# A two-layer MLP on one core: the opening reordered (smaller first loads, one more dummy matmul, half-width first tiles)

## The chip, the cores and the metric

The kernel runs on one core of one Trainium2 chip. The metric is the device time of one execution in microseconds (us). The profiled span is shorter than that time by about 1.8 us (132.8 against 134.6 in the same execution). Ratios below are the mean time of one kernel's fast runs over the mean time of the other's fast runs of the same rounds, on the same chip, so they are not quite the ratio of the medians that are quoted.

## The reference

```python
# x: (1, 2048, 640), w1: (640, 1728), w2: (1728, 640), all bf16
def reference(x, w1, w2):
    h = jnp.einsum("bsd,df->bsf", x, w1)
    h = jax.nn.silu(h)
    return jnp.einsum("bsf,fd->bsd", h, w2)
```

## The kernel before

The first layer needs x transposed (640 on the partitions). Rows are taken in four chunks of 512. The first chunk is loaded plainly and transposed on TensorE by matmuls against an identity; the other three come by transposing DMAs, which are issued some 1.3 us apart and land 2.8 us after their issue (from the trace), but have time. The 1728 columns of w1 (padded) give 14 tiles of 128, so the first layer is 4 x 14 groups of five 512-wide matmuls (280), each followed by a sigmoid on ScalarE and a multiplication on VectorE. The second layer is 448 matmuls. Before the first x arrives, five dummy matmuls on zeros keep TensorE occupied (1.19 to 3.50 us in the trace). PSUM is the memory that the matmuls write their results to. These are the parts that matter:

```python
w1_groups = [(0, 2), (2, 8), (8, FT)]      # weight tiles per DMA
N_WARM_MM = 5

@block.sync
def _(sp):
    hj = JB // 2                            # JB = 4 blocks of 128 rows
    sp.dma_start(out=x0_sb[:, 0:hj, :], in_=x0_v[:, 0:hj, :]).then_inc(sem_x0[0], 16)
    ...
    sp.wait_ge(sem_x0[1], 16)
    for gi in range(2, len(w1_groups)):
        load_w1_group(gi)
    ...
@block.scalar
def _(act):
    act.dma_start(out=x0_sb[:, hj:JB, :], in_=x0_v[:, hj:JB, :]).then_inc(sem_x0[1], 16)
    for gi in range(2):                     # w1 groups 0 and 1
        act.dma_start(...).then_inc(sem_w1[gi], 16)
    ...
@block.tensor
def _(pe):
    pe.wait_ge(sem_z, 1)
    for i in range(N_WARM_MM):              # dummies on zeros
        pe.matmul(ps1[:, NB1 - 1, :], lhsT=z_sb[:, 0:P], rhs=z_sb[:, :], start=True, stop=True)
    pe.wait_ge(sem_init, N_INIT)
    for j in range(JB):                     # 4 x 5 transposes
        if j % 2 == 0:
            pe.wait_ge(sem_x0[j // 2], 16)
        ...
    for sc in range(NSC):
        if sc == 0:                         # all four blocks copied out of PSUM
            pe.wait_ge(sem_tpc_v, JB)
            pe.wait_ge(sem_tpc_a, JB)
        ...
        for ft in range(FT):
            ...                             # 5 matmuls of 512 columns into ps1[:, buf, :]
```

## Time and profile before

Median 134.91 us in the first four runs. The profiled execution took 134.6 us.

| part of the profiled span (132.8 us) | us |
|---|---|
| up to the first real matmul | 7.55 |
| from there to the first matmul of the second layer | 61.64 |
| second layer, first to last matmul start | 60.80 |
| last matmul, copies, last store | 2.8 |

The page of the profile gives TensorE (PE) as the bound. The first line lists busy time per engine, the next two are the chain of work that ended last. PEld is TensorE's loading of weights, DVE VectorE, ACT ScalarE, POOL GpSimd, and SP the engine that issues most DMAs; L266 is line 266 of the kernel.

```profile
PE 126.5 (95%) x739; PEld 64.7 (49%) x753; DVE 51.6 (39%) x76; ACT 41.0 (31%) x77; POOL 1.6 (1%) x9
...
PE 94%; DMA 3%; issue 1%; DVE 0%; ACT 0%
PE ps L266 46%; PE ps L303 46%; DMA x_sb<-in_x_dram 3%; PE ps L240 2%; DVE xT_sb L384 0%; ACT o_sb L366 0%
```

A share of 95% seems to leave nothing. But busy is not the same as fast. The timeline of PE alone, over the first 13 us of the kernel before (start in us, duration, what, count, and in brackets the idle time ahead of it and what ended it), shows two gaps:

```profile
1.19 2.31 PE L224 MATMUL ps<-z_sb 128*128 128x512 bf16 x5 [1.19 <-DVE z_sb L379]
4.64 2.29 PE L240 MATMUL ps<-ident,x_sb 128*128 128x128 bf16 x20 [1.14 <-DMA x_sb<-in_x_dram]
7.55 5.68 PE L266 MATMUL ps<-xT_sb,w_sb 128*128 128x512 bf16 x20 [0.61 <-DVE xT_sb L384]
```

Dummies, then 1.14 us without x, then transposes, then 0.61 us until the last copy of transposed x is out of PSUM. The timeline of the weight loads (PEld, one per matmul) shows what the busy share hides. Each line is a load or a run of loads with no idle between:

```profile
8.79 0.15 PEld L266 LDWEIGHTS ps<-xT_sb,w_sb 128*128 128x128 bf16 x1 [0.28 <-issue]
9.21 0.15 PEld L266 LDWEIGHTS ps<-xT_sb,w_sb 128*128 128x128 bf16 x1 [0.28 <-issue]
9.64 0.15 PEld L266 LDWEIGHTS ps<-xT_sb,w_sb 128*128 128x128 bf16 x1 [0.28 <-issue]
10.05 1.39 PEld L266 LDWEIGHTS ps<-xT_sb,w_sb 128*128 128x128 bf16 x7 [0.26 <-issue]
```

Up to 9.64 the loads are 0.43 us apart, from 10.05 on about 0.216 us. The matmuls follow the same beat. So the first real matmuls ran at half speed although the clock row of the page reads full speed throughout. The packed trace does hold the step, in records that no view prints: its first record of the granted clock begins at 10.02 us, and the row counts as full whatever has no record. "Cold" and "released" below mean these two spacings.

The DMAs at the beginning (size, time from issue to landing; the two x loads were issued at 0.73 and 0.74 us):

```profile
x_sb<-in_x_dram SPq DMA_DIRECT2D x1, 320.0 KB, 3.8
x_sb<-in_x_dram ACTq DMA_DIRECT2D x1, 320.0 KB, 4.1
w_sb<-in_w_dram ACTq DMA_DIRECT2D x1, 320.0 KB, 4.6
```

### The profile page before, as it was taken

To read this page: it belongs to the slowest core of one execution; us is meant where nothing else is said; L and a number is where in the kernel's file an instruction comes from. 1 tells how busy PE (TensorE), PEld (TensorE's weight loads), DVE (VectorE), ACT (ScalarE), POOL (GpSimd) and SP (SyncE) were. 2 spreads that over 40 slices of the span, in tenths; PEclk is the share of its full clock that TensorE was granted. 3 is DMA by queue.
4 is the path that set the end of the run, shared out by engine and by line. 5 is a ranking of instruction groups with operands and counts; after the bars stand their busy time and mean duration, and the time that the engine had idled before them with its cause. 6 is when DMAs were issued, how large, how long until landed. Compare 5 with 4: busy or idle time off the path is not lost.

```text
span 132.8 us, 1833 instructions
## 1 busy us (share of the span) xinstructions
PE 126.5 (95%) x739; PEld 64.7 (49%) x753; DVE 51.6 (39%) x76; ACT 41.0 (31%) x77; POOL 1.6 (1%) x9
## 2 busy tenths in 40 slices
PE   6689999999999999999999999999999999999992
PEld 1624444444444444444445555555555555555461
DVE  0315666666666666666662222222012222220121
ACT  2525555555555555555550000000000000000001
POOL 4000000000000000000000000000000000000000
PEclk9999999999999999999999999999999999999999
DMA  4995444899300000000000111011111110111103
GB/s 104 354 362 140 102 102 97 274 378 141 73 2 0 0 5 2 0 0 0 0 0 5 49 49 49 14 35 54 49 49 49 49 54 7 42 49 49 54 0 99
DMA packets 15016, 9.78 MB, mean 74 GB/s; under 512 B 8800, under 2 KB 15008, under 8 KB 15008
## 3 DMA queue, kind: packets, MB, share of 16 engines
q1 hardware_dynamic: 13152, 7.97, 22.3%
q10 hardware_dynamic: 1856, 1.70, 4.0%
q8 instruction: 6, 0.10, 0.3%
q14 instruction: 2, 0.02, 0.0%
HBM read 5.08 MB, written 2.62 MB: 58 GB/s over the span
## 4 chain that ended last, share of the span: by engine, by line
PE 94%; DMA 3%; issue 1%; DVE 0%; ACT 0%
PE ps L266 46%; PE ps L303 46%; DMA x_sb<-in_x_dram 3%; PE ps L240 2%; DVE xT_sb L384 0%; ACT o_sb L366 0%
## 5 line engine op out<-in xcount | busy, mean ns | idle before, releaser
L266 PE MATMUL ps<-xT_sb,w_sb 128*128 128x512 bf16 x274 | 61.5, 384 | 0.9 <-DVE xT_sb L384 0.6
L303 PE MATMUL ps<-w_sb,hT_sb 128*128 128x512 bf16 (+1 forms) x440 | 60.6, 298 | 0.4
L393 DVE TENSOR_TENSOR hT_sb<-ps,sig_sb 128x512 bf16<-128x512 f32 x56 | 38.7, 691 | 24.6 <-ACT sig_sb L342 24.6
L303 PEld LDWEIGHTS ps<-w_sb,hT_sb 128*128 128x128 bf16 x448 | 34.5, 98 | 26.7
L266 PEld LDWEIGHTS ps<-xT_sb,w_sb 128*128 128x128 bf16 x280 | 27.6, 99 | 34.6 <-issue 1.7
L342 ACT ACTIVATE sig_sb<-ps 128x512 bf16<-128x512 f32 x56 | 33.4, 597 | 29.1 <-PE ps L266 29.1
L406 DVE CAST o_sb<-ps 128x512 bf16<-128x512 f32 x14 | 9.7, 692 | 42.9 <-PE ps L303 42.9
L354 ACT CAST o_sb<-ps 128x128 bf16<-128x128 f32 x14 | 3.7, 266 | 49.2 <-PE ps L303 49.2
L384 DVE CAST xT_sb<-ps 128x256 bf16<-128x256 f32 x4 | 1.7, 425 | 4.6 <-PE ps L240 4.3
L224 PE MATMUL ps<-z_sb 128*128 128x512 bf16 x5 | 2.3, 629 | 1.2 <-DVE z_sb L379 1.2
L240 PE MATMUL ps<-ident,x_sb 128*128 128x128 bf16 x20 | 2.3, 309 | 1.1 <-DMA x_sb<-in_x_dram 1.1
L418 DVE CAST o_sb<-ps 128x1024 bf16<-128x1024 f32 x1 | 1.2, 1225 | 5.3 <-PE ps L303 5.3
L240 PEld LDWEIGHTS ps<-ident,x_sb 128*128 128x128 bf16 x20 | 2.1, 143 | 2.0 <-issue 2.0
L366 ACT CAST o_sb<-ps 128x256 bf16<-128x256 f32 x1 | 0.4, 372 | 7.3 <-PE ps L303 7.3
L331 ACT CAST xT_sb<-ps 128x384 bf16<-128x384 f32 x4 | 1.9, 479 | 1.6 <-PE ps L240 1.5
L325 ACT ACT_TABLE_LOAD x1 | 1.3, 1283 | 2.4 <-issue 2.4
L224 PEld LDWEIGHTS ps<-z_sb 128*128 128x128 bf16 x5 | 0.6, 135 | 2.0 <-DVE z_sb L379 1.2
L153 POOL MEMSET w_sb<- 128x640 bf16 x1 | 0.6, 632 | 0.0
L379 DVE MEMSET z_sb<- 128x256 uint32 x1 | 0.3, 272 | 0.9 <-PEq L435 0.9
L150 POOL MEMSET w_sb<- 128x320 bf16 x1 | 0.4, 366 | 0.0
L140 POOL TENSOR_SCALAR_AFFINE_SELECT ident<-ident 128x128 bf16<-128x128 bf16 x1 | 0.3, 294 | 0.2 <-POOL ident L138 0.2
L325 ACT ACTIVATE warm_sb<-warm_sb 128x32 f32<-128x32 f32 x1 | 0.2, 230 | 0.0
(6 smaller groups left out, 0.7 us busy)
## 6 DMA issues: line engine op xcount, KB each, us to landing
out_dram<-o_sb SPq DMA_DIRECT2D x14, 160.0 KB, 1.8
w_sb<-in_w_dram SPq DMA_DIRECT2D x1, 1120.0 KB, 9.6
w_sb<-in_w_dram ACTq DMA_DIRECT2D x1, 960.0 KB, 7.2
w_sb<-in_w_dram SPq DMA_DIRECT2D x1, 960.0 KB, 7.0
w_sb<-in_w_dram SPq DMA_DIRECT2D x1, 880.0 KB, 6.3
x_sb<-in_x_dram SPq DMA_DIRECT2D x1, 320.0 KB, 3.8
x_sb<-in_x_dram ACTq DMA_DIRECT2D x1, 320.0 KB, 4.1
w_sb<-in_w_dram ACTq DMA_DIRECT2D x1, 320.0 KB, 4.6
```

The lines of the kernel that those rows point to most:

```text
L224: pe.matmul(ps1[:, NB1 - 1, :], lhsT=z_sb[:, 0:P], rhs=z_sb[:, :], start=True, stop=True,)
L240: ins = pe.matmul(tp_views[wv][:, sl, :], lhsT=x0_sb[:, j, dt * P:(dt + 1) * P], rhs=ident[:, :], start=True, stop=True,)
L266: ins = pe.matmul(ps1[:, buf, :], lhsT=w1_sb[:, dt, ft * P:(ft + 1) * P], rhs=xT_sb[:, dt, sc * SCH:(sc + 1) * SCH], start=(dt == 0), stop ...
L303: ins = pe.matmul(ps2[:, b2, c0:c0 + ncol], lhsT=hT_sb[:, ft, st * P:(st + 1) * P], rhs=w2_sb[:, ft, d0:d0 + ncol], start=(ft == 0), stop= ...
L325: act.activation(out=warm_sb[:, :], in_=warm_sb[:, :], func=ACT.Sigmoid)
L331: act.copy(out=xT_sb[:, TPV:DT, j * P:(j + 1) * P], in_=tp_views[wv][:, s0_:s0_ + (DT - TPV), :],).then_inc(sem_tpc_a, 1)
L342: act.activation(out=sig_sb[:, buf, :], in_=ps1[:, buf, :], func=ACT.Sigmoid,).then_inc(sem_act1, 1)
L354: act.copy(out=o_sb[:, ob, DA:D], in_=ps2[:, b2, c0:c0 + ncol]).then_inc(sem_ev_a, 1)
L384: dve.tensor_copy(out=xT_sb[:, 0:TPV, j * P:(j + 1) * P], in_=tp_views[wv][:, s0_:s0_ + TPV, :],).then_inc(sem_tpc_v, 1)
L393: dve.tensor_tensor(out=hT_sb[:, ft, sc * SCH:(sc + 1) * SCH], in0=ps1[:, buf, :], in1=sig_sb[:, buf, :], op=ALU.mult,).then_inc(sem_dve1, 1)
L406: dve.tensor_copy(out=o_sb[:, ob, 0:DA], in_=ps2[:, b2, c0:c0 + ncol]).then_inc(sem_ev_v, 1)
L418: dve.tensor_copy(out=o_sb[:, obA:obA + 2, 0:DA], in_=ps2[:, bA_, 0:2 * DA].rearrange("p (t c) -> p t c", t=2),).then_inc(sem_ev_v, 1)
```

## The change

The intent is to start the real matmuls earlier and to keep PE occupied from the start. Core of the diff, with lines shortened and joined (the loops over `units` on ScalarE and VectorE follow the one on PE; cut):

```diff
-    w1_groups = [(0, 2), (2, 8), (8, FT)]
+    w1_groups = [(0, 2), (2, 4), (4, 8), (8, FT)]
+    N_W1_ACT = 1                       # ACT issues group 0 only, SP the others
+    W1_BIG = 2
+    HN = SCH // 2
+    N_SPLIT_FT = 2                     # first two weight tiles in 256-column halves
+    units = [(0,0,0,HN), (0,1,0,HN), (0,0,HN,HN), (0,1,HN,HN), then 512-wide ...]
-    N_WARM_MM = 5
+    N_WARM_MM = 6
+    TP_BANKS = {0: (1, 0), 1: (1, 8), 2: (0, 8), 3: (1, 0)}   # transposes of block 3 reuse block 0's bank
+            pool.memset(z_sb[:, SCH // 2:SCH], 0.0).then_inc(sem_z, 1)   # POOL clears half of the zeros
-            sp.dma_start(out=x0_sb[:, 0:hj, :], in_=x0_v[:, 0:hj, :]).then_inc(sem_x0[0], 16)
+            for j in range(0, JB, 2):  # ACT likewise with j = 1, 3
+                sp.dma_start(out=x0_sb[:, j, :], in_=x0_v[:, j, :]).then_inc(sem_x0[j // 2], 16)
-            sp.wait_ge(sem_x0[1], 16)
+            sp.wait_ge(sem_x0[0], 32)
-                    pe.wait_ge(sem_tpc_v, JB)
-                    pe.wait_ge(sem_tpc_a, JB)
+                    jneed = (c0 + n - 1) // P + 1     # first halves need two blocks only
+                    pe.wait_ge(sem_tpc_v, jneed); pe.wait_ge(sem_tpc_a, jneed)
```

## The prediction

> **What bounds the kernel now.** TensorE. The engine summary has PE busy 126.5 of 132.8 us (95%); the chain of waits is 46% first-matmul line, 46% second-matmul line, 3% the DMA of the first x rows, 2% their transposes. From 7.55 to 130.2 us the chain shows only matmuls with 0.05 us issue gaps. So only the first 7.55 us and the tail can shrink; the change touches the beginning.
>
> **The beginning, from the timeline.** Five dummy matmuls run 1.19 to 3.50. PE then idles 1.14 us for x (two 320 KB loads, issued at 0.73, land 3.8 and 4.1 us later). Twenty transposes run 4.64 to 6.95, PE idles 0.61 us for the last copy, and real matmuls start at 7.55. The first six start 0.43 us apart, those after 10.05 us 0.216: 1.3 us lost to a slow PE. The clock row does not show it (it reads full); the spacing does. [...]
>
> **What the change does.**
> 1. x comes as four 160 KB loads, two per queue; the first two should land at about 3.6 us. In the window table the DMA has moved some 336 KB by 3.3 us and then runs at about 360 GB/s.
> 2. Warm-up starts 0.1 us earlier (memset halved over DVE and POOL) and gets a sixth matmul (+0.43 us): it ends at about 3.65, where x lands. The 1.14 us gap goes.
> 3. Transposes, still 20 at about 0.107 us: 3.65 to 5.8.
> 4. The first two weight tiles are multiplied in 256-column halves; the first half needs only the copies of blocks 0 and 1 (ready about 5.5), so the 0.61 us gap goes. Ten matmuls of 512 become twenty of 256; at 0.1 us each a weight load (98 ns) just hides. Cost under 0.1 us.
> 5. The first w1 load (landed about 5.9 before) becomes the likely last input: real matmuls start at about 6.0 instead of 7.55. The second group lands about 6.6, needed after 8; later loads have microseconds of slack.
>
> **Sum.** Start: -1.55 us. [...] Split: +0.1. All is on the critical path, since PE is gapless afterwards. Total about -2.5 us (-1.2 to -3.5). From 134.91: **132.4 us**, range **131.4 to 133.5**. The 2% limit lies at 132.2, so it is close: faster by over 2% 0.42, within 2% 0.57, slower 0.01.
>
> **What would show each step.** The chain's DMA and transpose part falls from 4.5% to about 3%; first real matmul at 5.8 to 6.3; no PE idle over 0.3 us after 1.2; fewer than six cold-spaced 512-column equivalents; the steady part unchanged (384 and 298 ns mean per matmul group; second-matmul phase 61.0 us).
>
> **What would make it wrong.** x or w1 landing late (more loads, 0.4 to 0.5 us issue each): start at 6.5 to 7, a gain of 1 us only. The clock released no earlier than 10 us: a gain of about 0.5 us, since work moved before it runs at half speed. Or released before 5 us: the transposes speed up too, and 131.5 is possible. The unchanged kernel's runs come in two values (134.6 and 135.2), which may be this release falling at different times; it blurs so small a difference.

The start (-1.55 us) and the split (+0.1) come to -1.45; the other 1.0 us of the total of 2.5 was the estimate of how much less would be lost to cold matmuls, and it rested on what no trace shows.

## The result, and the profile after

The changed kernel takes 132.12 us in the median (131.8 to 132.68, 11 runs) against 134.53 (133.4 to 135.24, 16 runs). The ratio is 0.9828 with a 95% interval of 0.9799 to 0.9856. Executions over 1.5% slower than the fastest of the same kernel are left out of the means. The interval straddles 0.98; the gain of about 2.3 us itself is clear of noise. The scatter shrank from 1.8 to 0.9 us. A later repeat of the unedited changed kernel (e9) gave 131.98 us and 0.9843.

The page of the kernel after, the same lines as above:

```profile
PE 125.2 (96%) x750; PEld 65.0 (50%) x764; DVE 51.5 (40%) x78; ACT 41.0 (32%) x79; POOL 1.9 (1%) x10
...
PE 94%; DMA 3%; issue 1%; ACT 0%
PE ps L334 46%; PE ps L297 46%; DMA x_sb<-in_x_dram 3%; PE ps L263 1%; ACT o_sb L395 0%
```

The page hardly differs. The timelines of PE and of its weight loads do:

```profile
1.10 2.74 PE L245 MATMUL ps<-z_sb 128*128 128x512 bf16 x6 [1.10 <-POOL z_sb L158]
4.13 1.79 PE L263 MATMUL ps<-ident,x_sb 128*128 128x128 bf16 x20 [0.29 <-DMA x_sb<-in_x_dram]
5.96 10.33 PE L297 MATMUL ps<-xT_sb,w_sb 128*128 128x256 bf16 x56
```

```profile
4.10 1.14 PEld L263 LDWEIGHTS ps<-ident,x_sb 128*128 128x128 bf16 x15 [1.17 <-issue]
5.45 0.29 PEld L263 LDWEIGHTS ps<-ident,x_sb 128*128 128x128 bf16 x5 [0.21 <-DVE xT_sb L413]
5.93 5.55 PEld L297 LDWEIGHTS ps<-xT_sb,w_sb 128*128 128x128 bf16 x37 [0.18 <-DVE xT_sb L413]
```

The first real matmul starts at 5.96 instead of 7.55 us. The last five transposes need 0.29 us, which is 58 ns each, about half of the cold 107 ns: the speed was released in the middle of the transposes, at 4.77 us by the clock record, and no real matmul was cold. The DMA table after:

```profile
x_sb<-in_x_dram SPq DMA_DIRECT2D x2, 160.0 KB, 3.2
x_sb<-in_x_dram ACTq DMA_DIRECT2D x2, 160.0 KB, 3.2
w_sb<-in_w_dram ACTq DMA_DIRECT2D x1, 320.0 KB, 4.2
```

**Where the time went.** The four parts of the span can be read from the timelines of every profiled execution. The second layer takes 60.80 us in each and the end 2.8, so the span is 63.6 plus the first two columns. With no cold matmul and no wait the first layer takes 60.43 us (without the halves) or 60.46 us (with them); what exceeds that is the loss. The two anchored runs e7 and e12 are left out of the table; their first layer takes 60.46 us too, after a start at 12.47 and 11.63 us.

| kernel | first real matmul (us) | first layer (us) | of it lost: cold | of it lost: waiting for w1 | span |
|---|---|---|---|---|---|
| before | 7.55 | 61.64 | 1.2 | | 132.8 |
| after | 5.96 | 60.46 | 0 | | 130.0 |
| e1 before, 8 dummies | 6.70 | 60.80 | 0 | 0.4 | 131.1 |
| e2 after, no dummies | 5.95 | 61.84 | 1.4 | | 131.4 |
| e3 after, no halves | 6.29 | 60.43 | 0 | | 130.3 |
| e4 after, x in two loads | 6.66 | 61.55 | 1.1 | | 131.8 |
| e5 after, 4 dummies | 5.93 | 60.75 | 0.3 | | 130.3 |
| e6 before, x in four loads | 6.89 | 60.92 | 0 | 0.5 | 131.4 |
| e8 after, old w1 groups | 7.27 | 61.17 | 0 | 0.7 | 132.1 |
| e9 after, unedited | 5.94 | 60.46 | 0 | | 130.0 |
| e10 after, 7 dummies | 5.95 | 60.46 | 0 | | 130.0 |
| e11 after, 8 early dummies | 6.17 | 60.72 | 0 | 0.3 | 130.5 |

So of the 2.8 us between the two profiled executions, 1.59 come from the start of the real matmuls and 1.18 from the cold loss. What this sum does not tell is the cause: the transposes, too, run at half or full speed (107 or 58 ns each), so part of the earlier start may itself be the earlier release. That is what the experiments take apart.

### The profile page after: what moved, and what is told of

Same layout as the page of the kernel before. It is cut to its first block, busy times and chain, and to the rows that moved or that the text cites. A ratio compares the mean times of both kernels' runs of the same rounds, so it can differ in the third digit from the quotient of the medians.

```text
span 130.0 us, 1869 instructions
## 1 busy us (share of the span) xinstructions
PE 125.2 (96%) x750; PEld 65.0 (50%) x764; DVE 51.5 (40%) x78; ACT 41.0 (32%) x79; POOL 1.9 (1%) x10
## 4 chain that ended last, share of the span: by engine, by line
PE 94%; DMA 3%; issue 1%; ACT 0%
PE ps L334 46%; PE ps L297 46%; DMA x_sb<-in_x_dram 3%; PE ps L263 1%; ACT o_sb L395 0%
## 5 line engine op out<-in xcount | busy, mean ns | idle before, releaser
L297 PE MATMUL ps<-xT_sb,w_sb 128*128 128x512 bf16 (+1 forms) x284 | 60.3, 371 | 0.3
L421 DVE TENSOR_TENSOR hT_sb<-ps,sig_sb 128x512 bf16<-128x512 f32 (+1 forms) x58 | 39.0, 673 | 22.5 <-ACT sig_sb L371 22.2
L297 PEld LDWEIGHTS ps<-xT_sb,w_sb 128*128 128x128 bf16 x290 | 28.3, 98 | 32.0 <-DVE xT_sb L413 0.2
L371 ACT ACTIVATE sig_sb<-ps 128x512 bf16<-128x512 f32 (+1 forms) x58 | 33.8, 583 | 26.9 <-PE ps L297 26.9
L263 PEld LDWEIGHTS ps<-ident,x_sb 128*128 128x128 bf16 x20 | 1.4, 113 | 1.4 <-issue 1.2
L263 PE MATMUL ps<-ident,x_sb 128*128 128x128 bf16 x20 | 1.7, 246 | 0.4 <-DMA x_sb<-in_x_dram 0.3
```

The source lines that it names most:

```text
L263: ins = pe.matmul(tp_views[wv][:, sl, :], lhsT=x0_sb[:, j, dt * P:(dt + 1) * P], rhs=ident[:, :], start=True, stop=True,)
L297: ins = pe.matmul(ps1[:, buf, 0:n], lhsT=w1_sb[:, dt, ft * P:(ft + 1) * P], rhs=xT_sb[:, dt, col0:col0 + n], start=(dt == 0), stop=(dt == ...
L371: act.activation(out=sig_sb[:, buf, 0:n], in_=ps1[:, buf, 0:n], func=ACT.Sigmoid,).then_inc(sem_act1, 1)
L421: dve.tensor_tensor(out=hT_sb[:, ft, col0:col0 + n], in0=ps1[:, buf, 0:n], in1=sig_sb[:, buf, 0:n], op=ALU.mult,).then_inc(sem_dve1, 1)
```

## The experiments

**Theory A.** A good part of the gain, perhaps half, is an earlier release of PE's speed, and it comes earlier because the change closes most of the idle gap of 1.14 us ahead of the transposes. How much work the release needs, and when it is then due, the author assumed; that is not shown by the runs. **Rival B.** Only the earlier availability of x and w1 counts; the release comes when it comes. Further rivals are named where they arise. The medians of before were 134.17 (e1 to e4), 134.87 (e5 to e8) and 134.05 (e9 to e12), so times are compared by their ratios to before.

### e1: the kernel before with 8 dummies

```diff
-    N_WARM_MM = 5
+    N_WARM_MM = 8
```

> The kernel before with 8 dummy matmuls instead of 5 and nothing else: they fill the 1.14 us in which PE waits for x. Theory A (part of the gain is an earlier release of the PE clock[...]): real matmuls still start at 7.5 to 7.7 us, but they are spaced 0.216 us from the start or nearly so, fewer than 3 of the cold 0.43 us spacings, and the time falls by 0.6 to 1.2 us against before (ratio 0.991 to 0.9955). Rival B (the gain is only the earlier start of the real matmuls; the release comes when it comes): no change or up to 0.1 us slower, six cold matmuls as before.

Measured: 132.90 us (132.69 to 133.35), ratio 0.9896 (0.9857 to 0.9934). One changed number gives 1.3 us, more than half of what the whole change gives. Timeline of PE:

```profile
1.18 3.39 PE L224 MATMUL ps<-z_sb 128*128 128x512 bf16 x8 [1.18 <-DVE z_sb L379]
4.50 1.28 PE L240 MATMUL ps<-ident,x_sb 128*128 128x128 bf16 x20
6.70 2.32 PE L266 MATMUL ps<-xT_sb,w_sb 128*128 128x512 bf16 x10 [0.93 <-ACT xT_sb L331]
9.22 2.12 PE L266 MATMUL ps<-xT_sb,w_sb 128*128 128x512 bf16 x9 [0.20 <-DMA w_sb<-in_w_dram]
```

The twenty transposes take 1.28 us instead of 2.29 and no real matmul is cold (ten in 2.32 us). The real matmuls start at 6.70, which neither theory had said: I had expected 7.5 to 7.7 and had forgotten that released transposes end earlier (0.14 us of the 0.85 us come from an earlier x in this execution). B is refuted. The gain was larger than A's 0.6 to 1.2 us for that reason. The last line shows the next limit: the third weight tile is now waited for.

### e2: the changed kernel without dummies

```diff
-    N_WARM_MM = 6
+    N_WARM_MM = 0
```

> The changed kernel without any dummy matmul. PE's first work is then the transposes at about 4.1 us. Theory A: real matmuls start at 6.2 to 6.5 us, [...]1.0 to 2.2 us of the gain are lost: 133.2 to 134.3. Rival B: the start of the real matmuls alone counts: 132.2 to 132.7.

Measured: 132.89 us (132.14 to 133.51), ratio 0.9881 (0.9839 to 0.9924). Timeline of PE:

```profile
3.86 2.29 PE L263 MATMUL ps<-ident,x_sb 128*128 128x128 bf16 x20 [3.86 <-DMA x_sb<-in_x_dram]
5.95 5.24 PE L297 MATMUL ps<-xT_sb,w_sb 128*128 128x256 bf16 x27
```

The real matmuls start at 5.95 us, the same as with dummies, yet 0.5 to 0.7 us are lost by the ratios and 0.8 by the medians, 1.4 in this profile, all of it as cold matmuls. This is the cleanest separation of the two causes: equal start, different release. The median lies between the two forecasts, below A's 133.2 and above B's 132.7. In the profile the release came 4.9 us after the first PE work (clock record at 8.76 us). That the loss by the medians is smaller than A had said I put down to executions with an earlier release, and to some loss in the changed kernel too; no profile shows either.

### e3: the changed kernel without the halves

```diff
-    N_SPLIT_FT = 2
+    N_SPLIT_FT = 0
```

> The changed kernel without the halves: all first-layer matmuls are 512 wide, so the first waits for the copies of all four x blocks. Both theories: PE idles some 0.5 to 0.6 us between the transposes and the first real matmul, real start at 6.5 to 6.7 instead of 5.96, time 0.4 to 0.6 us above the changed kernel (132.5 to 132.8). If the halves are worth nothing: 132.1.

Measured: 132.32 us (132.11 to 132.81), ratio 0.9851 (0.9815 to 0.9887), against 0.9828 and 0.9843 for the changed kernel: 0.1 to 0.3 us, less than expected and hardly clear of noise. Timeline of PE:

```profile
3.67 1.88 PE L263 MATMUL ps<-ident,x_sb 128*128 128x128 bf16 x20
6.29 4.91 PE L297 MATMUL ps<-xT_sb,w_sb 128*128 128x512 bf16 x22 [0.74 <-ACT xT_sb L362]
```

The expected gap is there (0.74 us), but x landed 0.5 us earlier in this execution than in that of the changed kernel, so the start moved by 0.33 us only. The halves are the smallest part of the change, and their gain is hardly shown.

### e4: the changed kernel with x in two loads

```diff
-            for j in range(0, JB, 2):
-                sp.dma_start(out=x0_sb[:, j, :], in_=x0_v[:, j, :]).then_inc(sem_x0[j // 2], 16)
+            sp.dma_start(out=x0_sb[:, 0:hj, :], in_=x0_v[:, 0:hj, :]).then_inc(sem_x0[0], 16)
             ...   # ACT likewise with blocks 2 and 3; waits for 16 instead of 32
```

> The changed kernel with x loaded as before, in two loads of 320 KB, everything else as changed. If the four smaller loads bring the earlier landing: first x block usable at about 4.5 instead of 4.0, real start at 6.4 to 6.5, time 0.3 to 0.6 us above the changed kernel (132.4 to 132.8), part of it from a gap of 0.7 us in front of the transposes that may delay the clock's release. If it is the first w1 load (landing at 5.9) that sets the start: 0 to 0.1 us.

Measured: 132.57 us over the four fast runs (131.85 to 133.59), ratio 0.987 (0.9811 to 0.9929). By the ratios 0.4 to 0.6 us are lost against the changed kernel, as expected. The median hides two groups: 131.85 and 131.93, and then 133.20 and 133.59, with nothing between; the two runs labelled slow (133.96 and 134.03, granted clock 1.0) lie just above the second. Timeline of PE, from the run at 133.59:

```profile
4.57 2.29 PE L263 MATMUL ps<-ident,x_sb 128*128 128x128 bf16 x20 [0.73 <-DMA x_sb<-in_x_dram]
6.66 4.51 PE L297 MATMUL ps<-xT_sb,w_sb 128*128 128x256 bf16 x24
```

Here the transposes are cold, the start is 0.7 us later, and half-width matmuls stay cold until 8.89 us (clock record). An idle gap of 0.73 us (0.94 by the spacing: the last dummy starts 2.11 us after the first and takes 0.43, the transposes start 3.48 after it) went with this late release, against 0.29 us and a release at 4.77 in the changed kernel. Why the runs fall into two groups with a hole between is not shown; I put it down to an early and a late release, but no run of the faster group was profiled. That group is as fast as the changed kernel (132.12), so there the earlier landing itself shows no gain; the smaller loads seem to pay through the gap that they close.

### e5: the changed kernel with 4 dummies

```diff
-    N_WARM_MM = 6
+    N_WARM_MM = 4
```

> The changed kernel with 4 dummy matmuls instead of 6, so that PE idles about 1.3 us between them and the transposes. Theory A, as the first four runs sharpened it: [...]four dummies are worth no more than none: [...]132.7 to 133.4, that is 0 to 0.4 us above the kernel without dummies (132.89) though it differs from the changed kernel by only two dummies. Rival C (each dummy helps in proportion, as a count of work): a third of the loss of 0.77, so about 132.4.

Measured: 132.76 us (132.07 to 133.44), ratio 0.9854 (0.9813 to 0.9896). The time lies in A's range, but this call's chip was also slower with the kernel before (134.87); by the ratio, 0.1 to 0.4 us are lost, which is Rival C's "a third of the loss". Between A and C this run is inconclusive. Its profile does not decide either: by the spacing, the release came at about 6.5 us (this trace holds no clock record), after an idle gap of 0.85 us ahead of the transposes, and 0.3 us were lost to cold matmuls.

### e6: the kernel before with x in four loads

```diff
-            sp.dma_start(out=x0_sb[:, 0:hj, :], in_=x0_v[:, 0:hj, :]).then_inc(sem_x0[0], 16)
+            for j in range(0, JB, 2):
+                sp.dma_start(out=x0_sb[:, j, :], in_=x0_v[:, j, :]).then_inc(sem_x0[j // 2], 16)
             ...   # ACT likewise with j = 1, 3; waits for 32
```

> The kernel before with x in four loads of 160 KB, nothing else changed (5 dummies, no halves, old w1 groups). x lands at 3.7 to 4.1 instead of 4.5, so the transposes start 0.4 to 0.8 us earlier and the idle gap before them shrinks from 1.14 to about 0.6. Theory A: [...]the release comes early in some of them and late in others: times spread over 2 us or more (131.9 to 134.5), median 132.5 to 133.8. Start-only view: a steady gain of 0.4 to 0.7 us with the spread of before: 133.5 to 134.

Measured: 133.85 us (132.9 to 134.82), ratio 0.9941 (0.9892 to 0.999). (In A's forecast, "some of them" are executions.) The scatter of 1.9 us is near A's 2 us, against 1.5 us of the kernel before in the same call; the median lies in the range of the start-only view and 0.05 us above A's. So the time alone does not decide. In the profiled execution (133.23 us) PE idled 0.49 us for x, no real matmul was cold, and 0.5 us went into waiting for the 768-column w1 load: one part of the change alone runs into what another part mends.

### e7 and e12: release out of the way, start hung on a DMA

If the scatter of before is the moment of release, a kernel in which the release is always over before the real work must scatter little. In e7 x is loaded behind w1, and 28 dummies bridge the time. In e12 x is loaded alone, after three w1 groups have landed and ahead of the fourth, with 22 dummies. Both are slower on purpose and correct.

```diff
-    N_WARM_MM = 6
+    N_WARM_MM = 22                          # e7: 28
+            load_w1_group(1); load_w1_group(2)
+            sp.wait_ge(sem_w1[2], 16)       # e7: SP waits for nothing, loads group 3 too, then x
             for j in range(0, JB, 2): ...   # x loads; ACT likewise after the same wait
+            sp.wait_ge(sem_x0[0], 32)
+            load_w1_group(3)
```

> Slower on purpose: the changed kernel with 28 dummy matmuls, and x loaded after w1 instead of ahead of it, so that it lands at about 9.5 to 11 us, [...]after the dummies are over. Everything real then runs at full clock, and its start hangs on a DMA alone. Theory A (the scatter of the kernel before, 133.4 to 135.2, is the moment of release): the scatter falls from 1.8 us to 0.5 us or less, and no real matmul is cold; time 136.5 to 138.5. Rival D (the scatter comes from the landing of DMAs or from elsewhere): it stays at 0.9 us or more.

> Slower on purpose, a mended form of the earlier anchored run: x is loaded alone, after the first three w1 groups have landed and ahead of the last, so that no other transfer competes with it; 22 dummies bridge to it (they end between 7 and 9 us, x lands at 8.3 to 9). All real matmuls warm. Theory A: scatter of 0.6 us or less, time 135.5 to 137. Rival D (scatter from elsewhere than the release): 1.0 us or more again.

Measured, e7: 138.43 us, four runs within 138.12 to 138.53 and two at 139.51 and 139.72. The expected 0.5 us of scatter was missed. The record lists a granted clock of 0.986 for the two outliers, and 0.999 to 1.0 for the other four. So the two ran at a lowered clock once more, for some 3.9 us if it was half speed (an estimate: 1.4% of their 137.8 us, doubled); where in the run is open, since the one profile is of another run. The four others scatter by 0.4 us, although x now landed behind the w1 loads (7.5 us after its issue on SP's queue, against 3.2 in the changed kernel).

Measured, e12: 137.58 us, all six runs within 137.48 to 137.78. The time is later than expected because the x that the transposes wait for landed at 10.1 us, not 8.3 to 9. The scatter of 0.3 us is what A had said, against 1.2 us of the kernel before in the same call. So with the release over and x loaded alone, the kernel is steady to 0.3 us; the scatter of before is not in the steady part, nor in the end. By itself e12 cannot tell the release from the landing of x, since it steadies both. The four runs of e7 at the full clock, steady to 0.4 us with x behind the w1 loads, speak against the landing.

The listed clocks of the kernel before bear on most of its range. Its trace (134.6 us) falls back to half clock at 132.90 us, 0.12 us past the span's end and 122.88 us after the release. Assume that the fall keeps this distance from the release. Only one trace of this kernel shows it; in the kernel after the distance is 126.29 us (4.77 to 131.07). Then in a run with an earlier release the fall comes earlier by as much, but the span ends earlier by only half as much, since cold work takes twice as long (0.43 against 0.216 us per matmul). In runs that are faster by more than 0.12 us, the fall should thus lie inside the span and lower the mean clock that the record lists. An estimate from these figures: 0.999 for runs of 134.08 to 134.35 us, 0.998 for 133.82 to 134.08. Of the 33 runs of the kernel before that list a clock, on three chips, twelve list less than 1.000: eight 0.999 (at 133.93, and at 134.05 to 134.35 us) and four 0.998 (133.97 to 134.05); two more of that range, at 134.27 and 134.34, list 1.000. All 14 runs from 134.58 us up list 1.000. Had they been late for another reason, with the release unmoved, the fall would lie inside the span of just these. So from 133.9 us up the listed clocks fit a time that follows the moment of release. The five runs below 133.82 list 1.000 again; the longer distance of the kernel after would do that, but no profile of such a run exists.

The two runs show one more thing. Their dummies run without a gap from 1.10 us on, as those of e1 do from 1.18. Weight loads of e7:

```profile
6.20 0.15 PEld L243 LDWEIGHTS ps<-z_sb 128*128 128x128 bf16 x1 [0.28 <-issue]
6.62 0.15 PEld L243 LDWEIGHTS ps<-z_sb 128*128 128x128 bf16 x1 [0.28 <-issue]
7.05 2.72 PEld L243 LDWEIGHTS ps<-z_sb 128*128 128x128 bf16 x13 [0.28 <-issue]
```

and of e1:

```profile
3.29 0.15 PEld L224 LDWEIGHTS ps<-z_sb 128*128 128x128 bf16 x1 [0.28 <-issue]
3.72 0.15 PEld L224 LDWEIGHTS ps<-z_sb 128*128 128x128 bf16 x1 [0.28 <-issue]
4.47 1.13 PEld L240 LDWEIGHTS ps<-ident,x_sb 128*128 128x128 bf16 x20 [0.60 <-issue]
```

The same unbroken stream of cold dummies was released at 4.24 us in e1 and only at 7.11 us in e7 and 7.13 in e12 (clock records; the loads above change their spacing between 3.72 and 4.47 us in e1, and from 7.05 on in e7), that is 3.1 and 6.0 us after its first matmul. A release that counted matmuls or time since the first one would have come at the same point. What does set the moment is not shown.

### e8: the changed kernel with the old w1 groups

```diff
-    w1_groups = [(0, 2), (2, 4), (4, 8), (8, FT)]
-    N_W1_ACT = 1
-    W1_BIG = 2
+    w1_groups = [(0, 2), (2, 8), (8, FT)]
+    N_W1_ACT = 2
+    W1_BIG = 1
```

> The changed kernel with w1 in the three old groups (256, 768 and 704 columns, the first two issued by ACT). The first-layer matmuls now reach the third weight tile at about 8.1 us, and the 768-column group landed at 9.0 to 9.2 in the kernel before and in the one with 8 dummies. If the finer groups are needed: PE waits 0.7 to 1.1 us there for w1, time 132.7 to 133.3. If they are not: 132.0 to 132.3.

Measured: 133.15 us over the five fast runs (132.94 to 133.84; the slow one, at 135.03, lists a clock of 0.987), ratio 0.9889 (0.9849 to 0.9929). That is in the range expected if the finer groups are needed. Timeline of PE:

```profile
3.91 1.90 PE L263 MATMUL ps<-ident,x_sb 128*128 128x128 bf16 x20
7.27 2.34 PE L297 MATMUL ps<-xT_sb,w_sb 128*128 128x256 bf16 x20 [1.46 <-DMA w_sb<-in_w_dram]
10.16 7.08 PE L297 MATMUL ps<-xT_sb,w_sb 128*128 128x512 bf16 x32 [0.55 <-DMA w_sb<-in_w_dram]
```

The expected wait at the third tile is there (0.55 us), and a larger one that I had not expected: the first group itself landed 5.5 us after its issue instead of 4.2, with the 960 KB load issued right behind it on the same queue. That load follows it in the kernel before, too, where the first group took 4.6 us, so what delayed it here is not shown. The finer groups are worth 0.6 to 0.8 us by the ratios and 1.0 by the medians; without them, much of what the earlier x brings is spent waiting for w1.

### e9, e10, e11: the reference again, 7 dummies, and 8 dummies that start earlier

```diff
 # e9: no edit
 # e10
-    N_WARM_MM = 6
+    N_WARM_MM = 7
 # e11
+    N_WARM_MM = 8
-            pe.wait_ge(sem_z, 2)
+            z_w = nc.const_aps.tensor(1.0, [P, P], bf16)      # exists before the body starts
+            z_m = nc.const_aps.tensor(1.0, [P, SCH], bf16)
-                    lhsT=z_sb[:, 0:P], rhs=z_sb[:, :],
+                    lhsT=z_w, rhs=z_m,
```

> The changed kernel itself, unedited, as the reference on the same chip for the three runs beside it, and as a second draw of the release time: 131.8 to 132.8, ratio 0.978 to 0.987; first real matmul at 5.9 to 6.3 us[...].

> The changed kernel with 7 dummies, which end at about 4.1 us, where x lands, so that no idle is left before the transposes. Theory A: no worse than the changed kernel, 0 to 0.2 us faster[...]. If it is 0.3 us or more slower, the seventh dummy holds up transposes whose x had landed.

> An attempt at something better: the changed kernel with 8 dummies that read a constant which exists before the kernel body starts (a one-element column read 128 and 512 times over), so they need no memset and start at about 0.75 instead of 1.10 us. Theory A: [...]worth 0 to 0.3 us: 131.7 to 132.3. If dummies past the landing of x hold up the transposes: 0.1 to 0.3 us slower.

Measured: e9 131.98 us (131.73 to 132.17), ratio 0.9843 (0.9814 to 0.9873); e10 131.96 us (131.59 to 132.35), ratio 0.9841; e11 131.99 us (131.84 to 132.32), ratio 0.9847. The three are the same. Filling the gap ahead of x wholly, or starting the dummies 0.33 us earlier, buys nothing more. Timeline of PE in e11:

```profile
0.77 3.27 PE L246 MATMUL ps<-const-bfloat16-1.0 128*128 128x512 bf16 x8 [0.77 <-PEq L464]
3.94 1.54 PE L264 MATMUL ps<-ident,x_sb 128*128 128x128 bf16 x20
6.17 11.03 PE L298 MATMUL ps<-xT_sb,w_sb 128*128 128x256 bf16 x59 [0.70 <-ACT xT_sb L363]
```

The release came at 3.60 us (clock record), the transposes were over by 5.5 us, and then PE idled 0.70 us. The view names a copy that ended then, but the first half-width matmul needs the copies of blocks 0 and 1 only, and what it also needs, the first w1 load, was issued at 1.68 us and took 4.4, so it came in at about 6.1, right ahead of the start at 6.17. I infer that this load is where the start sits now; in the changed kernel, too, it lands at 5.82 us (trace), 0.14 us ahead of the start, and the transposes start just as long after the landing of x that they wait for (0.13 us both before and after). No version was found that beats the changed kernel.

## Why the prediction was right

The time (132.4 predicted, 132.12 measured, range 131.4 to 133.5), the start of the real matmuls (6.0 predicted, 5.96 measured) and the cold loss (1.0 us less estimated, 1.18 less measured) came out as said, and the call that 2% would be a close thing did too. Point by point:

- **Bound and critical path.** Right. Second layer (60.80 us) and end (2.8) are the same in all profiles; every gain and loss lies ahead of the release or in waits for w1.
- **x lands at 3.6.** It was 4.0 in the profiled run, and PE still idled 0.29 us. So the DMA and transpose part of the chain fell from 4.5% to 3.8%, not to 3%. Over the profiles with the four loads, PE got its x between 3.67 and 4.13 us.
- **Transposes all at 0.107 us, until 5.8.** In the profiled run 13 of 20 ran at half of that. This made up for the late x. In e9, x came at 3.96, nearly all transposes were cold, and the start was 5.94: several chains (transposes, copies, first w1 load) end within 0.2 us of each other, so that the start stays at 5.9 to 6.0 over the changed kernel, e2, e5, e9 and e10. The right sum was partly luck of two errors, partly this.
- **The first w1 load as the likely last input.** In e11 it comes in right ahead of the start, and in e8, where it is later, PE waits 1.46 us for it. In the changed kernel it lands 0.14 us ahead of the start, together with the last copies. Right as one of several limits.
- **The second w1 group lands at 6.6.** It was issued at 4.0 us and took 3.4, so about 7.4, where 8.1 is needed. Right in effect, but the slack was 0.7 us, not 1.5.
- **Halves take away the 0.61 us gap.** The gap went, but without the halves the loss is 0.1 to 0.3 us (e3), not 0.6.
- **The cold loss.** The estimate left 0.3 us of it. In the profiles the release came at 4.8 us in the first, 5.8 in e9 (by the spacing) and 5.4 in e10 (clock record), where it had been 10.0 in the kernel before, and the cold loss went wholly. That the release comes earlier once the gap of 1.14 us is filled, e1 shows with one number changed: at 4.24 us, and no real matmul was cold. The author's reason for the size of the estimate was not shown.
- **The split between the causes.** The prediction booked 1.55 us for the start and 1.0 for the speed. As a sum over the timeline this is what was measured. As causes it is not: e1 moves the start by 0.85 us by nothing but dummies, mostly because released transposes end sooner. Keeping PE occupied alone gives 1.3 us; the loads, the groups and the halves give the rest, and each of them alone less than its share, since they wait for one another. Two small parts were not tested alone: the halved memset (the dummies start 0.09 us earlier) and the new order of the PSUM banks, for which the last five transposes wait 0.2 us for a copy in the profile.

## What to carry to other kernels

When an engine reads 95% busy, look at the spacing of its instructions in the first 10 us, and count the idle gaps ahead of the first real work: here one number, dummies long enough to reach the landing of the first input, was worth 1.3 us. Where the dummies stopped 0.73 us short of it in the profiled run (e4), the fast runs fell into two groups, 131.9 and 133.2 to 133.6 us. Once a start is pulled forward, the next load in line has to come with it; test every part of such a change both alone in the old kernel and taken out of the new one, because parts that unblock each other look small alone. Where a kernel scatters by more than the effect sought, find what the scatter is before comparing medians.
